# RetNet attention with a PReLU MLP on one core: a planner that counts TensorE's instruction chunks, three early transfers in flight, and 64-wide products with the sums

## The chip, the cores and the metric

The kernel runs on 1 core of a Trainium2 chip. The metric is the device time of one execution in microseconds. The engines are TensorE (PE; its weight loads are shown apart as PEld), VectorE (DVE), ScalarE (ACT), GpSimd (POOL) and SyncE (SP), which here issues the transfers between the chip's memory and the core.

## The reference, cut to what matters

```python
def _attn_ref(q, k, v):                    # each (8, 8, 576, 64): batch, heads, sequence, head size
    scores = 1.0 / np.sqrt(D_) * np.matmul(q, k.transpose(0, 1, 3, 2))
    gamma = 1.0 - 2.0 ** (-5.0 - np.arange(H))
    rel = pos[:, None] - pos[None, :]
    Dmat = np.where(rel >= 0, gamma[:, None, None] ** rel[None, :, :], 0.0)
    return np.matmul(scores * Dmat, v)

x = attn_out.transpose(0, 2, 1, 3).reshape(4608, 512)
h = x @ w_in                               # (512, 2048)
g = np.maximum(h, 0.0) + alpha * np.minimum(h, 0.0)
out = g @ w_out                            # (2048, 512)
```

Everything is float32.

## The kernel before

**Attention by chunks.** The sequence of 576 is cut into 9 chunks of 64. Inside a chunk, the scores of queries and keys are masked and multiplied with the values. Across chunks, the products of keys and values are summed into a running state for each head, and a chunk's queries are multiplied with the sum of all chunks before it. Two heads make a pair, since a head is 64 wide and an engine's tile has 128 rows.

**Two ways through the attention.** The first two of the eight batches are done in *parts*, all heads at once, while the machine starts: parts 0, 1, 2 are chunks 0 to 3, 4 to 7 and 8 of batch 0, and parts 3, 4, 5 those of batch 1. A part has these steps, each a function of the kernel:

- `load_part`: loads of k, q, v, 128 rows by 512 each (256 KB).
- `part_scale`: GpSimd scales q and v (L424).
- `part_transposes`: TensorE turns k and q (L448), ScalarE copies them out (L454).
- `part_scores`: 32 products of 64 x 64 on TensorE (L472), VectorE masks them (L478).
- `part_states`: 32 products of keys and values (L494), VectorE sums them up (L506, L508), and `part_carry` hands the last sum to the next part (L514).
- `part_values`: 32 products of masked scores and values (L541), then, added to the same two accumulators, the products with the sums (L557). These are cut into two halves of the head, so that each gives 32 rows: 64 products in parts 1 and 4, 48 in parts 0 and 3 (their first chunk has no sum before it). ScalarE copies the two accumulators into the x of the MLP (L572).
- Parts 2 and 5 have one chunk and go through `last_part` (L593 to L631).

The other six batches go pair by pair, 24 *joint steps* (`joint`), spread between the work of the MLP from 105 us on. TensorE's work in a joint step is: the values of the pair before in two pieces, `v0` and `v1` (L809, 18 products together); the last chunk's scores, `x` (L860, 2 products); and scores and states of the pair, `su` (L867 and L870, 32 products). `on_pe` gives them to the planner as the groups of `GROUPS`.

**The MLP.** Tokens go in 18 blocks of 256, hidden units in 8 groups of 256. The first eight cells (a block and a group) run in plain float32 (`unit_plain`, L1039, then `second_plain`, L1070). All others run as products of split pieces (`unit`, L1108; `unit_two`, L1138, two blocks at once; `second`, L1189), for which ScalarE, VectorE and GpSimd split x, g and the weights. Every product of plain float32 shows as two weight loads and two matmuls in the trace, a product of pieces or a transpose as one of each.

**Weights.** Each of 32 weight tiles of 512 KB is loaded, turned into float32 by ScalarE (L670, L672), VectorE (L680, L682, L691) and GpSimd (L694) in `convert`, and used from there.

**The order.** The code lists operations with `do(engine, cost, function, reads, writes, ...)`. `plan()` then makes the order: first backwards, for a due time of each operation, then forwards. There it takes, among operations of an engine that could start within `SLACK` of the earliest, the one that is due first. `SWITCH` is added where an operation's kind differs from the last one on the engine. The order is fixed by this plan; on the chip each engine runs its own list, with semaphores where one engine needs another's result. Costs change the order alone.

**Transfers.** All go through SP's queue, in the order of the plan (`dma`). For the operations that the plan puts into the first 100 us, a transfer on SP also waits until the bytes in flight before it, with its own, are under `IN_FLIGHT`: `5 << 18` bytes, five transfers of 256 KB.

Of the kernel before, what the change touches and what calls it, by code (L numbers as in the profile page):

```python
# [21 lines left out]
def kernel(  # L22
# [72 lines left out]
    a16 = const.tile([NFC, P], FP32, name="a16")  # L95
    malpha = const.tile([P, NFC], FP32, name="malpha")

    gam = [1.0 - 2.0 ** (-5.0 - h) for h in range(H)]
# [54 lines left out]
    class Op:  # L153
        def __init__(self, eng, cost, fn, deps, banks, late, lock, hold):
            self.eng, self.cost, self.fn, self.deps = eng, cost, fn, deps
            self.banks, self.late, self.lock, self.hold = banks, late, lock, hold
            self.n = len(ops)

# [17 lines left out]

    def do(eng, cost, fn, r=(), w=(), late=0.0, lock=False, kind=None, hold=0.0):
        deps, gens = set(), []
        for keys, writes in ((r, False), (w, True)):
            for g, *sub in keys:  # L180
                wr, rd = g.keys.setdefault(tuple(sub), ([], []))
                deps.update(wr)
                if writes:
                    deps.update(rd)
                deps.update(g.before)
                if g not in gens:
                    gens.append(g)
        op = Op(eng, cost, fn, None, [g.slot for g in gens if g.slot and g.slot.bank], late, lock, hold)
        for g, *sub in w:
            g.keys[tuple(sub)] = ([op], [])  # L190
        for g, *sub in r:
            g.keys[tuple(sub)][1].append(op)
        for g in gens:
            assert not g.slot or g.slot.gen is g
            g.ops.append(op)
        op.deps = [d for d in deps if d is not op]
        op.gens, op.kind = gens, kind or eng
        ops.append(op)
        return op
# [19 lines left out]
    flight, now = [], [0.0]  # L219
    LIMITED, IN_FLIGHT = 100.0, 5 << 18  # L220

    LAT = {"PE": 0.2}

    def plan():
# [42 lines left out]
        free, held, port, wire, kinds = dict(BEGIN), {}, [0.0, ""], 0.0, {e: e for e in BEGIN}  # L267
        can = [0.0] * len(ops)
        for op in ops:
            if not op.deps:  # L270
                ready[op.eng].append(op)

        def earliest(op):
            t = max(free[op.eng], can[op.n], op.hold)
            for b in op.banks:
                if b in held:
                    t = max(t, max([x + LAT.get(e, 0.1) for e, x in held[b].items()
                                    if e != op.eng] or [0.0]))
            if op.lock and port[1] != op.eng:
                t = max(t, port[0])  # L280
            if op.late:
                t = max(t, wire - BACKLOG, due[op.n] + last - HOLD)
            return t + SWITCH.get(op.eng, 0.0) * (kinds[op.eng] != op.kind)

        while len(order) < len(ops):
# [18 lines left out]
            kinds[op.eng] = op.kind  # L304
            free[op.eng] = end[op.n] = t + op.cost
            if op.late:
                wire = max(wire, t + op.cost) + op.late
                end[op.n] = wire
# [13 lines left out]

    AHEAD_PE = 150
    BACKLOG, HOLD = 2.0, 30.0
    LAG, HOLD_X = 2, 100.0
    PUMP0, PUMP = ((1, 1), (0, 1), (0, 1), (0, 1)), ((1, 2), (1, 2), (0, 1), (0, 1))
    GROUPS = (("v0",), ("v1",), ("x", "su"))
    SLACK, SWITCH = {"PE": 0.3}, {"PE": 0.1}
    BEGIN = {"PE": 3.8, "ACT": 0.5, "DVE": 5.5, "POOL": 5.4, "SP": 0.5}
# [106 lines left out]
    def part_transposes(x, i, bank):  # L436
# [6 lines left out]
        for m in range(2):  # L443
            pt = Gen(next(bank))

            def f(m=m, pt=pt):
                for c in range(NPAIR):
                    nc.tensor.transpose(pt.get()[:, c * P:(c + 1) * P],  # L448
                                        part(x, i)[:, m, 2 * c:2 * c + 2].rearrange(
                                            "p h d -> p (h d)"), ident)  # L450
            do("PE", 0.6 if x else 1.0, f, [key_p(x, i, m)], [(pt, 0)])

# [5 lines left out]
    def part_scores(x, bank):  # L458
# [7 lines left out]
        for m in range(2):  # L466
            def f(m=m):
                for c in range(NPAIR):
                    for p2 in range(2):
                        for h2 in range(2):  # L470
# [3 lines left out]
                                kT()[half(h2), c, j], qT()[half(h2), c, j], start=True, stop=True)  # L474
            do("PE", 0.6, f, [(kt, "t", m), (qt, "t", m)], [(ps[0], m), (ps[1], m)])
        for h2 in range(2):
# [7 lines left out]
    def part_states(x, bank):  # L484
# [4 lines left out]
        for m in range(2):  # L489
            def f(m=m):  # L490
                for c in range(NPAIR):
                    for p2 in range(2):
                        for h2 in range(2):
# [5 lines left out]
                                             skip_group_check=True)  # L499
            do("PE", 0.6, f, [key_p(x, 0, m), key_p(x, 2, m)], [(pu[0], 0), (pu[1], 0)])  # L500
        for j in range(4):
# [25 lines left out]
    def part_values(x, bank):  # L527
# [7 lines left out]
        for m in range(2):  # L535
            def f(m=m):
                for c in range(NPAIR):
                    for p2 in range(2):
                        for h2 in range(2):
# [5 lines left out]
                                             skip_group_check=True)  # L545
            do("PE", 0.6, f, [key_p(x, 2, m), (a, "m", 0), (a, "m", 1)], [(pv[0], 0), (pv[1], 0)])
        for m in range(2):
            js = [j for j in (2 * m, 2 * m + 1) if j or x % 3]

            def f(js=js):  # L550
                for j in js:
                    su = sums_of(x, j - 1) if j else carry_of(x)
                    for c in range(NPAIR):
                        for h2 in range(2):
                            for e in range(0, D, 32):
# [4 lines left out]
                                                 stop=(j >= 2), skip_group_check=True)  # L560
            do("PE", 1.0 if len(js) > 1 else 0.6, f, [(qt, "t", m)] + [
                sums_key(x, j - 1) if j else carry_key(x) for j in js], [(pv[0], 0), (pv[1], 0)])

# [15 lines left out]
    def last_part(x):  # L579
# [9 lines left out]
        def f():  # L589
            to = pt.get().rearrange("p (i c s) -> p i c s", i=2, c=NPAIR)  # L590
            for i in range(2):
                for c in range(NPAIR):
                    nc.tensor.transpose(to[:, i, c], part(x, i)[0:C, 0, 2 * c:2 * c + 2].rearrange(  # L593
                        "p h d -> p (h d)"), ident[0:C, 0:C])
        do("PE", 0.8, f, [key_p(x, 0, 0), key_p(x, 1, 0)], [(pt, 0)])
        do("ACT", 0.59, lambda: nc.scalar.copy(
# [6 lines left out]
        def f():  # L603
            for c in range(NPAIR):
                for h2 in range(2):
                    nc.tensor.matmul(sc(h2)[:, c], tt()[half(h2), 0, c], tt()[half(h2), 1, c],
                                     start=True, stop=True)
        do("PE", 0.5, f, [(t, "t")], [(ps[0], 0), (ps[1], 0)])
        for h2 in range(2):
# [5 lines left out]
        def f():  # L615
# [6 lines left out]
            for c in range(NPAIR):  # L622
                for h2 in range(2):
                    for e in range(0, D, 32):
# [3 lines left out]
                                         skip_group_check=True)  # L628
        do("PE", 0.9, f, [key_p(x, 2, 0), (t, "m", 0), (t, "m", 1), (t, "t"), carry_key(x)], [(pv, 0)])
        gx, o = chunk_home(x, NJ - 1)  # L630
# [203 lines left out]
    def on_pe(parts, groups):  # L834
        for some in groups:
            do("PE", sum(parts[x][0] for x in some), lambda some=some: [parts[x][1]() for x in some],
               [key for x in some for key in parts[x][2]],
               [key for x in some for key in parts[x][3]])

# [187 lines left out]
    def unit_plain(cell):  # L1027
# [5 lines left out]
        for cc in range(2):  # L1033
            def mm(cc=cc):
                w = plain[4 * u + cc]
                for f in range(2):
                    for c2 in range(2):
# [5 lines left out]
                                         stop=(cc == c2 == 1), skip_group_check=True)  # L1043
            do("PE", 1.75, mm, keys + [plain[4 * u + cc]], [(ph, 0)])
        do("ACT", 0.62, lambda: nc.scalar.activation(
# [10 lines left out]
    def second_plain(cell):  # L1056
# [9 lines left out]
        for m in range(2):  # L1066
            def mm(m=m, a=acc):
                for f in range(2):
# [4 lines left out]
                                     stop=(cell["last"] and f == 1))  # L1073
            do("PE", 1.75, mm, [(ga, 0), (ga, 1), plain[4 * u + 2], plain[4 * u + 3]],
               [(acc[m], 0)])
            if cell["last"]:
# [12 lines left out]
    def unit(cell):  # L1089
# [7 lines left out]
        for f in range(2):  # L1097
# [5 lines left out]
            def mm(f=f, at=at):  # L1103
# [7 lines left out]
            do("PE", 1.43, mm, x_keys(vis, side) +  # L1111
               [w_at[u, i][l] for i in range(2) for l in range(3)], [(ph, 0), (ph, 1)], kind="pieces")
            fc = 2 * u + f
# [14 lines left out]
    def unit_two(va, vb, u, ga, f):  # L1128
# [3 lines left out]
        def mm():  # L1132
# [7 lines left out]
        do("PE", 2.73, mm, x_keys(va, 0) + x_keys(vb, 1) +  # L1140
           [w_at[u, i][l] for i in range(2) for l in range(3)], [(p0, 0), (p1, 0)], kind="pieces")
        fc = 2 * u + f
# [31 lines left out]
    def second(cell):  # L1174
# [7 lines left out]
        for m in range(2):  # L1182

            terms = ((0, 0), (0, 1)), ((1, 2),)
            for some in reversed(terms) if cell["last"] else (sum(terms, ()),):
                def mm(m=m, a=list(acc), some=some):
# [8 lines left out]
                   [w_at[u, i][l] for i in (2, 3) for _, l in some],  # L1195
                   [(acc[2 * m + b], 0) for b in sorted({b for b, _ in some})], kind="pieces")
            if cell["last"]:
# [331 lines left out]
```

## Time and profile before

| what | us |
|---|---|
| median of 3 runs (lowest, highest) | 937.26 (936.19, 939.43) |
| the profiled execution's own time | 939.56 |
| its span, first to last instruction | 937.9 |
| TensorE idle before its first matmul | 4.24 |
| products of pieces with w_out, L1189: matmuls busy | 344.7 |
| products of pieces with w_in, L1108: matmuls busy | 208.7 |

Matmuls overlap, so their busy times are no sum of a time line. The profile's page gives busy time by engine, TensorE's granted clock and the share of the 16 DMA engines in 40 slices, the traffic of each DMA queue (q1 is the program's data, q8 and q14 fetch instructions), and the chain of work that ended last. "Issue" is a wait for which the profile has no releaser. In the page, DMA engines are busiest in the first 15% of the span:

```
DMA  9987487798888869965335421121212122221112
q1 hardware_dynamic: 235424, 119.59, 50.3%
q8 instruction: 65, 1.06, 0.5%
q14 instruction: 35, 0.29, 0.1%
```

The chain of work that ended last is 92% TensorE: 38% L1189, 21% L1108, 18% L1138.

### The profile page before, as it was taken

To read this page: it belongs to the slowest core of one execution; us is meant where nothing else is said; L and a number is where in the kernel's file an instruction comes from. 1 tells how busy PE (TensorE), PEld (TensorE's weight loads), DVE (VectorE), ACT (ScalarE), POOL (GpSimd) and SP (SyncE) were. 2 spreads that over 40 slices of the span, in tenths; PEclk is the share of its full clock that TensorE was granted. 3 is DMA by queue.
4 is the path that set the end of the run, shared out by engine and by line. 5 is a ranking of instruction groups with operands and counts; after the bars stand their busy time and mean duration, and the time that the engine had idled before them with its cause. 6 is when DMAs were issued, how large, how long until landed. Compare 5 with 4: busy or idle time off the path is not lost.

```text
span 937.9 us, 21264 instructions
## 1 busy us (share of the span) xinstructions
PE 915.6 (98%) x8241; PEld 778.5 (83%) x8241; DVE 531.9 (57%) x1070; ACT 552.8 (59%) x1175; POOL 578.8 (62%) x491
## 2 busy tenths in 40 slices
PE   6799999999999999999999999999999999999998
PEld 5576688988898898889899988888888888888887
DVE  6668566666776666766654764443444444444333
ACT  4366556566766665666775885645546463635342
POOL 5657766739676685664666465748374656647363
PEclk9999999999999999999999999999999999999999
DMA  9987487798888869965335421121212122221112
GB/s 233 226 200 137 131 197 159 157 205 188 196 189 197 204 152 196 196 148 151 113 113 191 125 90 68 46 90 45 90 45 91 58 89 88 78 71 45 45 45 68
DMA packets 235524, 120.94 MB, mean 129 GB/s; under 512 B 203408, under 2 KB 203424, under 8 KB 235424
## 3 DMA queue, kind: packets, MB, share of 16 engines
q1 hardware_dynamic: 235424, 119.59, 50.3%
q8 instruction: 65, 1.06, 0.5%
q14 instruction: 35, 0.29, 0.1%
HBM read 74.19 MB, written 31.98 MB: 113 GB/s over the span
## 4 chain that ended last, share of the span: by engine, by line
PE 92%; SPq 2%; DMA 2%; issue 1%; DVE 1%; POOL 1%; ACT 1%; POOLq 0%; ACTq 0%; DVEq 0%
PE pso L1189 38%; PE psh L1108 21%; PE psh L1138 9%; PE psa L1138 9%; PE psh L1039 3%; PE pso L1070 3%; PE psh L809 3%; SPq L206 2%; PE psa L870 2%; DMA op<-in_moe_w_out_dram 1%; DMA kn<-in_k_dram 1%; PE psh L860 1%; PE psa L867 1%; DMA w<-in_q_dram 1%; PE psa L472 0%
## 5 line engine op out<-in xcount | busy, mean ns | idle before, releaser
L1189 PE MATMUL pso<-w,g 128*128 128x512 f32 x1416 | 344.7, 391 | 0.0
L1189 PEld LDWEIGHTS pso<-w,g 128*128 128x128 f32 x1416 | 260.2, 188 | 50.6
L1108 PE MATMUL psh<-lx,w 128*128 128x256 f32 x1608 | 208.7, 285 | 0.0
L1108 PEld LDWEIGHTS psh<-lx,w 128*128 128x128 f32 x1608 | 202.0, 191 | 7.2 <-issue 0.5
L1168 POOL TENSOR_TENSOR g<-g 128x512 fp32r<-128x512 f32 x136 | 176.1, 1295 | 23.0 <-DVE w L1014 4.4
L1165 POOL TENSOR_TENSOR g<-ga,g 128x512 fp32r<-128x512 f32 x72 | 93.0, 1292 | 110.1 <-ACT g L1161 90.1
L1116 DVE SCALAR_TENSOR_TENSOR ga<-psh,ga 128x256 f32<-128x256 f32 x144 | 60.6, 421 | 67.5 <-ACT ga L1115 66.1
L1115 ACT COPY ga<-psh 128x256 f32<-128x256 f32 x144 | 53.6, 373 | 70.7 <-PE psh L1108 61.5
L1165 POOL TENSOR_TENSOR g<-x,g 128x512 fp32r<-128x512 f32 x40 | 51.7, 1294 | 63.8 <-ACT g L1161 61.3
L1122 DVE SCALAR_TENSOR_TENSOR ga<-psh,malpha,ga 128x256 f32<-128x256 f32 x144 | 68.9, 478 | 24.2 <-ACT psh L1119 23.4
L1018 POOL TENSOR_TENSOR lx<-lx 128x512 fp32r<-128x512 f32 x48 | 61.9, 1294 | 27.3 <-DVE lx L1014 12.7
L1119 ACT ACTIVATE psh<-ga 128x256 f32<-128x256 f32 x144 | 56.0, 389 | 28.0 <-DVE ga L1116 27.8
L1161 ACT ACTIVATE g<-ga 128x512 fp32r<-128x512 f32 x72 | 45.5, 632 | 25.0 <-DVE ga L1122 16.9
L1165 POOL TENSOR_TENSOR g<-vn,g 128x512 fp32r<-128x512 f32 x24 | 31.1, 1296 | 42.1 <-ACT g L1161 38.9
L888 DVE SCALAR_TENSOR_TENSOR at<-psa,pf,mask 64x512 f32<-64x512 f32 x48 | 36.0, 750 | 34.8 <-PE psa L867 33.9
L1163 ACT ACTIVATE g<-ga 128x512 fp32r<-128x512 f32 x72 | 45.0, 625 | 0.0
L1207 DVE TENSOR_TENSOR op<-pso,op 128x512 f32<-128x512 f32 x34 | 23.4, 687 | 36.5 <-PE pso L1189 36.4
L1161 ACT ACTIVATE g<-x 128x512 fp32r<-128x512 f32 x40 | 25.2, 632 | 32.0 <-PE pso L1189 16.1
L1145 DVE SCALAR_TENSOR_TENSOR x<-psh,x 128x512 f32<-128x512 f32 x20 | 13.8, 690 | 44.5 <-PE psh L1138 40.9
L809 PEld LDWEIGHTS psh<-at,vn 128*64 128x64 f32 x864 | 28.2, 137 | 12.6 <-issue 5.3
L1014 POOL TENSOR_TENSOR lx<-x,lx 128x512 fp32r<-128x512 f32 x24 | 31.0, 1294 | 12.2 <-DVE wa L682 6.2
L809 PE MATMUL psh<-at,vn 128*64 128x64 f32 x864 | 32.7, 226 | 2.5 <-DMA vn<-su 1.3
(289 smaller groups left out, 1695.5 us busy)
## 6 DMA issues: line engine op xcount, KB each, us to landing
xk<-x SPq DMA_DIRECT2D x18, 512.0 KB, 4.0
out_dram<-o SPq DMA_DIRECT2D x36, 256.0 KB, 4.2
ok<-o SPq DMA_DIRECT2D x34, 256.0 KB, 2.8
x<-xk SPq DMA_DIRECT2D x17, 512.0 KB, 5.0
op<-ok SPq DMA_DIRECT2D x17, 512.0 KB, 3.9
qx<-in_q_dram SPq DMA_DIRECT2D x96, 72.0 KB, 3.1
kx<-in_k_dram SPq DMA_DIRECT2D x96, 72.0 KB, 3.0
kn<-in_k_dram SPq DMA_DIRECT2D x48, 144.0 KB, 3.8
```

Source lines behind the costliest of these rows:

```text
L809: nc.tensor.matmul(pv[i].get()[half(h2), (j - js[0]) * C:(j - js[0] + 1) * C], vns[n % 2][:, h2, j], mt.get()[:, h2, j], start=True, stop= ...
L1018: lambda l=l, d=d, h=view(0, c): nc.gpsimd.tensor_tensor(out=piece(d()), in0=h(), in1=l(), op=ALU.subtract),
L1108: nc.tensor.matmul(at(b), w[:, c0:c0 + P], xp(l, cc), start=(n == 0 and cc == 0), stop=(n > 0 and cc == NCC - 1), skip_group_check=True)
L1115: do("ACT", 0.36, lambda g=g, at=at: nc.scalar.copy(g(), at(1)), [(ph, 1)], [(ga, f)])
L1116: do("DVE", 0.42, lambda g=g, at=at: nc.vector.scalar_tensor_tensor(out=g(), in0=at(0), scalar=ONE, in1=g(), op0=ALU.mult, op1=ALU.subtrac ...
L1119: do("ACT", 0.39, lambda g=g, at=at: nc.scalar.activation(at(1), g(), ACTF.Relu, scale=-1.0), [(ga, f)], [(ph, 1)])
L1122: do("DVE", 0.48, lambda g=g, at=at, fc=fc: nc.vector.scalar_tensor_tensor(out=g(), in0=at(1), scalar=malpha[:, fc:fc + 1], in1=g(), op0=A ...
L1138: nc.tensor.matmul(p.get(), w[:, c0:c0 + P], piece(words_of(g)[:, o:o + DM]), start=(l != 1 and cc == 0), stop=(l > 0 and cc == NCC - 1))
L1161: do("ACT", 0.64, lambda: nc.scalar.mul(piece(to.get()[:, 2]), whole(), BELOW), both, [(to, 2)])
L1165: do("POOL", 1.29, lambda: nc.gpsimd.tensor_tensor(out=piece(to.get()[:, 1]), in0=whole(), in1=to.get()[:, 2], op=ALU.subtract), both + [( ...
L1168: do("POOL", 1.29, lambda: nc.gpsimd.tensor_tensor(out=piece(to.get()[:, 2]), in0=to.get()[:, 0], in1=to.get()[:, 1], op=ALU.subtract), [( ...
L1189: nc.tensor.matmul(a[2 * m + b].get(), piece(g.get()[:, l, f, m * P:(m + 1) * P]), w_piece(u, 2 + f, l), start=(cell["first"] and f == 0 a ...
```

## The change

- The planner's forward pass gets a model of how TensorE's instructions arrive. Operations on TensorE carry a `size`, their number of matrix instructions. `at[0]` counts them modulo `CHUNK` = 256, beginning at 66; when an operation crosses a boundary, the next boundary may not be crossed before `FETCH` = 3.1 us (and up to 0.8 more while transfers are under way) have passed.
- Small products are a kind of their own (`kind="small"`), costs of several TensorE operations are set anew, and `SLACK` of TensorE goes from 0.3 to 0.2.
- `IN_FLIGHT` goes from `5 << 18` to `3 << 18`.
- In parts 1, 3 and 4 (`wide`), the products with the sums are no longer cut into halves of 32 rows: 32 products in parts 1 and 4, 24 in part 3. Before them ScalarE copies one row's two elements out of the accumulator that has the values (`spy`), and the first wide product waits for that copy, by a dependency added by hand.

```diff
+    spy = const.tile([1, 2], FP32, name="spy")
...
-    LIMITED, IN_FLIGHT = 100.0, 5 << 18
+    LIMITED, IN_FLIGHT = 100.0, 3 << 18
...
+        at = [CHUNK - 190, 0.0]
...
+            if op.size and at[0] + op.size > CHUNK:
+                t = max(t, at[1] - op.cost * (CHUNK - at[0]) / op.size)
             return t + SWITCH.get(op.eng, 0.0) * (kinds[op.eng] != op.kind)
...
+            if op.size:
+                at[0] += op.size
+                if at[0] >= CHUNK:
+                    at[0] -= CHUNK
+                    over = end[op.n] - op.cost * at[0] / op.size
+                    at[1] = over + FETCH + min(max(wire - over, 0.0), 0.8)
...
+    CHUNK, FETCH = 256, 3.1
...
-    SLACK, SWITCH = {"PE": 0.3}, {"PE": 0.1}
+    SLACK, SWITCH = {"PE": 0.2}, {"PE": 0.1}
...
-            do("PE", 0.6 if x else 1.0, f, [key_p(x, i, m)], [(pt, 0)])
+            do("PE", 0.52 if x else 1.0, f, [key_p(x, i, m)], [(pt, 0)], size=8)
...
-            do("PE", 0.6, f, [(kt, "t", m), (qt, "t", m)], [(ps[0], m), (ps[1], m)])
+            do("PE", 0.58, f, [(kt, "t", m), (qt, "t", m)], [(ps[0], m), (ps[1], m)], kind="small",
+               size=64)
...
+        wide = x > 0
+        if wide:
+            def f():
+                seen[:] = [nc.scalar.copy(spy[0:1], to(1)[0:1, NPAIR - 1, :, 0])]
+            seen = []
+            do("ACT", 0.2, f, [(pv[0], 0), (pv[1], 0)], [(pv[0], 1)])
         for m in range(2):
             js = [j for j in (2 * m, 2 * m + 1) if j or x % 3]
+
+            def g(js=js):
+                for c in range(NPAIR):
+                    for j in js:
+                        su = sums_of(x, j - 1) if j else carry_of(x)
+                        for h2 in range(2):
+                            ins = nc.tensor.matmul(
+                                to(j % 2)[half(h2 ^ (j % 2)), c, j // 2], su[half(h2), c],
+                                qT()[half(h2), c, chunk(j)], start=False, stop=(j >= 2),
+                                skip_group_check=True)
+                            if seen:
+                                tc.add_manual_dep(ins.ins, seen.pop().ins.name, mybir.DependencyInfo(
+                                    mybir.DependencyClass.Sync, mybir.DependencyReason.DATA),
+                                    reason="rows")
...
-            do("PE", 1.0 if len(js) > 1 else 0.6, f, [(qt, "t", m)] + [
-                sums_key(x, j - 1) if j else carry_key(x) for j in js], [(pv[0], 0), (pv[1], 0)])
+            do("PE", (0.29 if wide else 0.5) * len(js), g if wide else f, [(qt, "t", m)] + [
+                sums_key(x, j - 1) if j else carry_key(x) for j in js] + wide * [(pv[0], 1)],
+               [(pv[0], 0), (pv[1], 0)], kind="small", size=(32 if wide else 64) * len(js))
...
             do("PE", sum(parts[x][0] for x in some), lambda some=some: [parts[x][1]() for x in some],
                [key for x in some for key in parts[x][2]],
-               [key for x in some for key in parts[x][3]])
+               [key for x in some for key in parts[x][3]], kind="small",
+               size=sum(136 if x == "su" else 72 if x[0] == "v" else 0 for x in some))
...
-            do("PE", 1.75, mm, keys + [plain[4 * u + cc]], [(ph, 0)])
+            do("PE", 1.86, mm, keys + [plain[4 * u + cc]], [(ph, 0)], size=16)
...
-            do("PE", 1.75, mm, [(ga, 0), (ga, 1), plain[4 * u + 2], plain[4 * u + 3]],
-               [(acc[m], 0)])
+            do("PE", 1.86, mm, [(ga, 0), (ga, 1), plain[4 * u + 2], plain[4 * u + 3]],
+               [(acc[m], 0)], size=8)
```

The products of pieces get sizes of 24 (L1108, L1138) and 4 a term (L1189). Lines move by the added code; L448, L472, L494, L541, L557, L809, L1039, L1070, L1108 and L1189 of before are L461, L485, L508, L556, L597 (and the wide products L581), L851, L1082, L1113, L1151 and L1232 after; the copy is L570.

## The prediction

> **What bounds the kernel now.** I began with busy times and waits. TensorE is busy nearly throughout, and its waits are few, so the time is TensorE's own work plus its gaps.
>
> ```profile
> PE 915.6 (98%) x8241; PEld 778.5 (83%) x8241; DVE 531.9 (57%) x1070; ACT 552.8 (59%) x1175; POOL 578.8 (62%) x491
> ```
>
> ```profile
> PE psa L557 <- issue: 4.1, 1, 4.1
> PE psh L809 <- DMA vn<-su: 1.3, 1, 1.3
> PE psh L557 <- issue: 1.3, 1, 1.3
> ```
>
> The first line is the page's; the others are waits of the matmul engine. "Issue" is a wait that no semaphore explains. Both issue waits stand inside L557, the products with the sums. The chain of waits around the longer one, and then stretches of time (busy, matmuls, granted clock, DMA share, GB/s):
>
> ```profile
> 33.62 0.27 PE psh L557 x15
> 33.90 0.06 PE psh L557 x3
> 33.96 4.06 issue
> 38.02 0.48 PE psa L557 x20
> 38.67 0.33 PE psh L557 x22
> 39.00 3.61 PE psh L1039 x8
> ...
> 43.24 1.93 PE psh L1039 x8
> ```
>
> ```profile
> 39.00:42.40 3.40, 3.40 (x8) 0.50 0.96 240
> ...
> 86.00:92.00 6.00, 4.71 (x198) 1.00 0.55 100
> ```
>
> Two things are to be seen: 4.06 us of nothing, and after it eight matmuls in 3.61 us that take 1.93 four microseconds later, because the clock was 0.50 for 3.40 us. After the short wait at 89.94 the clock stayed 1.00.
>
> What TensorE waited for is told by the instruction queue: 65 packets with 1.06 MB, 16 KB each, for some 16,500 matrix instructions, so about 256 a packet. The engine counts up to the two waits are 602 + 602 and 1488 + 1489; their difference, 1773, and the 19 semaphore instructions of the program between them make 7 x 256. Both waits stand at such a boundary.
>
> ```profile
> q1 hardware_dynamic: 1164, 0.29, 125.3%
> q8 instruction: 1, 0.02, 5.7%
> ```
>
> These are the DMA queues at 35.2 to 36.6: the chunk's packet moves only there, with the data queue full. One chunk earlier the boundary fell at 31.9 (third matrix instruction of L541). From crossing to going on took 6.1 us (31.9 to 38.02), and TensorE had 2.0 us of small products for it. At 88.2 it took 3.0 (88.23 to 91.23), with the data queue at 20.6%, against 1.7 us of products.
>
> **The change, part by part.**
>
> *Counting chunks.* I laid the same boundaries (every 256 instructions, first at the 194th) on the changed order. No chunk there is pure small products. The densest in the disturbed stretch holds 11 instructions of L508, 4 matmuls of L1082 (1.83 us, half of the 16-matmul row of 3.65), all of L556 (128 instructions, 1.09 us) and 99 of L581 (0.85), with the new wait (0.6) inside: 4.5 us. That is above 3.0 and below 6.1. I take the wait as gone (the nearest row, with fewer loads in the way, is 3.0): -4.06 and -1.29. With it goes the half clock, half of 3.40: -1.7. If the fetch still takes 6.1, 1.6 us stay.
>
> The Trainium skill speaks against this: "Runtime: NRT & Kernel Launch", section on instruction fetch mechanics, calls the fetch of a 16 KiB block mostly hidden, so counting would bring nothing. The trace shows two waits at just these boundaries, and it decides. "TensorE: Matmul & The Clock Gate", Part 1, says an idle window of some 3.4 us halves the clock; our rows agree for 4.06 (0.50) and for 1.29 (1.00), and the 1.7 us are from the rows.
>
> *64-wide products.* 11 blocks (4 + 3 + 4) go from 16 products of 32 columns to 8 of 64; each is two matmuls. L557 in part 3 ran undisturbed: 96 matmuls in 1.32 us (63.83 to 65.15), 13.75 ns each. A 64x64 product in the same four quarters is L541: 64 in 1.09, 17 ns. So 352 x 13.75 = 4.84 becomes 176 x 17 = 2.99: -1.85. Other bound: L619, 64x64 in two quarters, 16 in 0.61 us, 38 ns: 6.7 us, +1.85. I take the first, same shape and same quarters but for one operation.
>
> *The new copy and wait.* In parts 3 and 4 the changed order puts two products of L1113 (1.91 us) between L556 and the wide products; they hide the copy. In part 1 the wide products stand straight behind L556: TensorE, with everything in its queue, waits for the copy. A small ScalarE copy is 0.2 us, plus two hand-overs of 0.1 to 0.2: +0.6 (0.3 to 1.0). Without the cover, parts 3 and 4 would cost the same each.
>
> *Order of the rest.* The added sizes and kinds, the smaller slack and the new costs run no instruction, but they move TensorE's operations for the whole kernel. The count gives 72 to each of the two halves of the values (L851), which together are 18 products of two matmuls, 72 instructions. The planner so sees 280 instructions in a joint step of 208, and puts other work inside. In the changed order TensorE enters the joint products from the split-precision ones 33 times after the first, now 26. The price of an entry, from the chain:
>
> ```profile
> 144.61 3.12 PE psh L1108 x24
> 147.73 2.75 PE pso L1189 x12
> 150.47 2.87 PE psh L1108 x24
> ...
> 156.09 1.20 PE psh L809 x36
> ```
>
> ```profile
> 196.31 0.73 PE psh L809 x20
> ...
> 198.24 0.62 PE psh L809 x16
> ```
>
> From start to next start in the timeline, 24 matmuls of L1108 behind joint products take 2.97 (118.47) to 3.02 (144.54), else 2.87: 0.13 on the mean. L1189 before them lasts 2.84, else 2.75: 0.09. Values in two pieces take 0.73 + 0.62, in one 1.20: 0.15. Sum 0.37; 7 x 0.37 = +2.6. Early, the plain units are entered 22 times, now 19; L1070 before small products takes 1.91, between transposes 1.72: 3 x 0.19 = +0.6.
>
> *Three transfers in flight.* A 256 KB load alone took 3.3 us, the next ones 4.0, 4.6 and 4.8, and they landed 1.19 apart. With three allowed, a turn is the longer of 3 x 1.19 = 3.57 and 3.3 + 0.4 (issue, 0.43 on SP): 3.7 us for 786 KB, 212 GB/s; before it averaged 235 in 0 to 33.96. All on SP shift: the fourth load, now behind the first landing (4.11), lands 0.3 later, about 8.0, and the last transposes of part 0 with it; weights behind it by 2 us, which VectorE's and ScalarE's queue meets with its own wait for the sums (L506 at 15.3). In part 1 the last block of q lands near 24, its scaling (1.04) waits behind POOL's conversions until 25.5, and TensorE waits 1.2 for it; but 2.4 us of waits in the same stretch now (0.33 for L454, 0.66 for malpha, 1.07 for the masked scores, 0.33 for x) partly go, since 16 transposes stand together. I take +0.5, between -1.5 (the waits go) and +9 (priced below).
>
> *Sum:* -4.06 - 1.7 - 1.29 - 1.85 + 0.6 + 2.6 + 0.6 + 0.5 = -4.6. The profiled execution has a span of 937.9 and took 939.56, above the median of 937.26 (936.19 to 939.43); so 933.3 in the span and **932.7** for the median.
>
> **Rivals.**
>
> *A, the stall stays in part (18%).* For it: the fetch of 31.9 stood in a full data queue, and three loads still fill it. The chunk of 4.5 us then leaves 1.6 idle. Idle of 1.29 did not halve the clock, 4.06 did; with 1.7 for the clock, -4.6 + 3.3 = -1.3: 936.0. Against it: fewer packets in front of it.
>
> *B, the window starves TensorE (12%), slower.* Place: states of part 1 (L508), which need the 23rd transfer, 6.3 MB into the stream. TensorE would be there near 32 us; 6.3 MB at 212 GB/s plus 2 is 31.7. It decides from 3.7 us a load on. If a load takes 4.5 even with three in flight (the page's median for k), a turn is 4.9, 160 GB/s: 41 us, 9 late: 932.7 + 9 = 941.7. Against it: the first load's 3.3, and weights that landed 0.7 apart.
>
> *C, more is gained (12%).* The split values hide the 1.3 us for vn<-su and the 1.0 for ga, and the start gains 1.5 instead of losing 0.5: -4.3 more, 928.4.
>
> **How the numbers follow.** The forecast holds 58%, from -2.5 to -6.5. No change is within 0.3% (2.8 us; 934.4 to 940.1), about what a measurement can tell. Faster: 53 of the forecast's 58, 11 of C, 1 of A: 65. Same: 5 of the forecast, 15 of A, 1 each of B and C: 22. Slower: 11 of B, 2 of A: 13. The range takes the forecast and most of A and C: 928.8 to 937.6; the likeliest alone 930.8 to 934.8.
>
> **What would show it.** Issue waits of L581 gone, clock 1.00 after the start; 96 and 128 wide-product instructions in 0.8 and 1.1 us; a wait of 0.6 on L570's copy in part 1 alone; L1151 at 3.1 seven times more often. Waits of TensorE for k, q, v or converted weights above 3 us before 45 us would be B; an issue wait near 36 us would be A. The forecast is wrong if TensorE's gaps before 110 us add up to more than now, 15.7 with the first 4.2.

## The result, and the profile after

| | median, us (runs) | ratio to the kernel before, 95% interval |
|---|---|---|
| before | 936.67 (17) | |
| after | 941.16 (17) | 1.0046 [1.0033, 1.006] |

The changed kernel is slower by 4.5 us. The forecast was 932.7. The profiled execution of after took 942.04 with a span of 940.3, 0.9 above its median; that of before stood 2.9 above its own median, so the two traces are 2.5 us apart, not 4.5.

First the lines that answer to those of before: busy times from the page, then TensorE's waits (us in total, times, longest), then stretches of time (length, busy, matmuls, granted clock, DMA share, GB/s).

```profile
PE 920.1 (98%) x8065; PEld 778.8 (83%) x8065; DVE 532.0 (57%) x1070; ACT 551.8 (59%) x1178; POOL 579.2 (62%) x491
```

```profile
PE psh L1082 <- ACT x L613: 2.5, 1, 2.5
PE psh L1082 <- POOL lx L736: 1.6, 1, 1.6
PE psa L556 <- DVE w L523: 1.6, 1, 1.6
...
PE psa L581 <- ACT spy L570: 0.3, 1, 0.3
```

```profile
20.40:23.80 3.40, 3.40 (x10) 0.50 0.75 171
37.50:40.90 3.40, 3.40 (x16) 0.50 0.78 159
68.20:71.60 3.40, 3.40 (x22) 0.50 0.66 166
86.00:92.00 6.00, 6.00 (x81) 1.00 0.82 153
```

What is to be seen: both issue waits of before are gone. Three waits stand in their place, at 16.89, 35.6 and 65.3, and each has a half-clock stretch of 3.4 us behind it, where before had one such stretch. The wait for the spy copy is there in part 1 alone, 0.3 and not 0.6.

The trace is one execution, and three such stretches are not the rule. One stretch of 3.41 us at half clock takes 0.0018 off the mean granted clock, which is on record for each of the 17 executions: 0.994 for this one, 0.996 or 0.997 for five, 0.998 for eight, 1.000 for three.

By stage, from TensorE's instructions ("waits" are its idle gaps behind its first matmul, "joint" from the first joint step to the first product of two blocks):

| profiled execution | first joint step at | waits before it | half-clock stretches before it | joint | waits in joint | rest |
|---|---|---|---|---|---|---|
| before | 104.95 | 11.4 | 1 | 451.9 | 2.5 | 381.0 |
| after | 106.66 | 10.5 | 3 | 453.2 | 1.7 | 380.5 |

Before the first joint step the waits became shorter by 0.9 us, but two more half-clock stretches cost 2 x 1.7 = 3.4 us; the first warm-up of the clock was some 0.7 us cheaper. That makes +1.8; +1.7 was measured. In the joint stretch the waits fell by 0.8 and TensorE's work grew by 2.1.

What the new waits wait for is told by the engines' own lists. ScalarE in after, from the timeline (start, duration, engine, line, operation; idle time before it and its releaser in brackets), and the same in a kernel that differs in the number of transfers in flight alone (five; the first experiment below):

```profile
15.19 0.68 ACT L712 ACTIVATE qT<-lx 128x512 f32<-128x512 f32 x1 [1.83 <-DMA lx<-in_moe_w_in_dram]
...
17.50 1.75 ACT L613 COPY x<-pso 128x512 f32<-128x512 f32 x3
```

```profile
16.01 0.67 ACT L714 ACTIVATE lx<-lx 128x512 int32<-128x512 uint32 x1
17.41 1.77 ACT L613 COPY x<-pso 128x512 f32<-128x512 f32 x3 [0.73 <-PE pso L597]
```

The copies L613 hand the x of part 0 to TensorE's L1082. They stand behind weight conversions (L712, L714). In after one of these waits 1.83 us for its load. TensorE is done with its products (L597) at 16.4, but ScalarE can start the copies only at 17.50. With five in flight ScalarE is through with the weights at 16.7 and waits for TensorE. This first wait costs next to nothing beside five, though: there TensorE came to L597 1.4 us later (its clock rose at 14.11, in after at 10.17), and the copies start at 17.41, hardly earlier.

At 35.6 TensorE waits for converted weights themselves. VectorE's and GpSimd's steps of that conversion in after, then with five:

```profile
32.53 0.69 DVE L722 TENSOR_SCALAR psa<-w 128x512 f32<-128x512 f32 x1 [2.65 <-ACT w L712]
...
35.87 1.29 POOL L736 TENSOR_TENSOR lx<-lx,w 128x512 int32<-128x512 int32 x1 [2.29 <-DVE lx L733]
```

```profile
27.99 0.69 DVE L722 TENSOR_SCALAR psa<-w 128x512 f32<-128x512 f32 x1 [0.20 <-ACT w L712]
...
31.81 1.29 POOL L736 TENSOR_TENSOR lx<-lx,w 128x512 int32<-128x512 int32 x1 [1.59 <-issue]
```

VectorE has to wait 2.65 us for ScalarE's part (L712) and begins 4.5 us later than with five, GpSimd's last step (L736) 4.1 us later. TensorE is 0.9 us later before this wait and 3.5 behind it.

At 65.3 it waits for the sums of part 3 (L521, L523), which stand on VectorE behind conversions (L722, L724, L733):

```profile
58.13 0.66 ACT L712 ACTIVATE w<-w 128x512 f32<-128x512 f32 x1 [2.14 <-POOL w L437]
...
58.83 0.69 DVE L722 TENSOR_SCALAR psa<-w 128x512 f32<-128x512 f32 x1 [5.47 <-ACT w L712]
...
65.33 0.42 DVE L521 COPY w<-psa 128x256 f32<-128x256 f32 x1
...
66.88 0.33 PE L556 MATMUL psa<-at,w 64*64 64x64 f32 x4 [1.59 <-DVE w L523]
```

```profile
51.02 0.67 ACT L712 ACTIVATE w<-w 128x512 f32<-128x512 f32 x1
...
51.72 0.69 DVE L722 TENSOR_SCALAR psa<-w 128x512 f32<-128x512 f32 x1 [3.85 <-ACT w L712]
...
58.23 0.42 DVE L521 COPY w<-psa 128x256 f32<-128x256 f32 x1
```

From L722 to L521 VectorE takes 6.5 us in both, without a pause; what differs is when it can begin. In after a load of w_in lands at 58.06 and ScalarE's L712 starts at 58.13, with five at 51.02. The products that L521 reads were done by 63.4 (L508 in the timeline); TensorE needs their accumulator again for the next values (L556) and waits until 66.9.

TensorE's plain products (L1082, L1113) come in the same order in both kernels, so each can be set against itself:

| TensorE starts | after | five in flight | later by |
|---|---|---|---|
| first L1082, behind the wait at 16.89 | 19.39 | 19.33 | 0.06 |
| first of the eight L1082 before the wait at 35.6 | 31.70 | 30.76 | 0.94 |
| next L1082, behind that wait | 37.21 | 33.67 | 3.54 |
| next L1113, behind the half-clock stretch | 43.30 | 38.40 | 4.90 |
| an L1082 before the wait at 65.3 | 60.75 | 55.90 | 4.86 |
| an L1113 behind it | 68.56 | 61.31 | 7.25 |
| an L1082 behind the half-clock stretch | 74.02 | 65.28 | 8.74 |
| first joint step | 106.66 | 97.09 | 9.57 |

So 7.8 of the 9.6 us come between 31 and 74 us, with the waits at 35.6 and 65.3 and the clock behind them; 0.9 come with the clock behind the first wait, and 0.8 later.

### The profile page after: what moved, and what is told of

Same layout as the page of the kernel before. It is cut to its first block, busy times and chain, and to the rows that moved or that the text cites. A ratio compares the mean times of both kernels' runs of the same rounds, so it can differ in the third digit from the quotient of the medians.

```text
span 940.3 us, 20910 instructions
## 1 busy us (share of the span) xinstructions
PE 920.1 (98%) x8065; PEld 778.8 (83%) x8065; DVE 532.0 (57%) x1070; ACT 551.8 (59%) x1178; POOL 579.2 (62%) x491
## 4 chain that ended last, share of the span: by engine, by line
PE 52%; DVE 0%; issue 0%
PE pso L1232 26%; PE psh L1181 9%; PE psa L1181 9%; PE psh L1151 7%; DVE o L1255 0%; PE psh L851 0%
## 5 line engine op out<-in xcount | busy, mean ns | idle before, releaser
L1232 PE MATMUL pso<-w,g 128*128 128x512 f32 x1416 | 346.0, 392 | 0.0
L1232 PEld LDWEIGHTS pso<-w,g 128*128 128x128 f32 x1416 | 260.0, 188 | 51.0
L1151 PE MATMUL psh<-lx,w 128*128 128x256 f32 x1608 | 208.6, 285 | 0.9 <-ACT x L870 0.9
L1151 PEld LDWEIGHTS psh<-lx,w 128*128 128x128 f32 x1608 | 202.2, 191 | 8.0 <-ACT x L870 1.0
L851 PEld LDWEIGHTS psh<-at,vn 128*64 128x64 f32 x864 | 28.3, 137 | 12.0 <-issue 4.7
L1181 PE MATMUL psh<-w,w 128*128 128x512 f32 x144 | 34.6, 389 | 0.0
```

The lines of the kernel that those rows point to most:

```text
L1151: nc.tensor.matmul(at(b), w[:, c0:c0 + P], xp(l, cc), start=(n == 0 and cc == 0), stop=(n > 0 and cc == NCC - 1), skip_group_check=True)
L1181: nc.tensor.matmul(p.get(), w[:, c0:c0 + P], piece(words_of(g)[:, o:o + DM]), start=(l != 1 and cc == 0), stop=(l > 0 and cc == NCC - 1))
L1232: nc.tensor.matmul(a[2 * m + b].get(), piece(g.get()[:, l, f, m * P:(m + 1) * P]), w_piece(u, 2 + f, l), start=(cell["first"] and f == 0 a ...
```

## The experiments

Each ratio is against the kernel before on the same chip (medians 936.91, 935.75 and 936.35 in the three groups, the first two on one chip); a difference to after or to five in flight is one of medians. The kernel before itself moved by 1.2 us between groups, so where two kernels stand in different groups, about 1 us can't be told.

**Five in flight again.** The order of the plan does not depend on the window, so this undoes that part alone.

```diff
-    LIMITED, IN_FLIGHT = 100.0, 3 << 18
+    LIMITED, IN_FLIGHT = 100.0, 5 << 18
```

> The changed kernel with five transfers in flight again; every engine runs the same instructions in the same order. Theory W (the window of three makes the weights late, and with them the conversions that stand in order on ScalarE, VectorE and GpSimd): the waits of 2.50 us at 16.9, 1.60 at 35.6 and 1.59 at 65.3 go or halve, two of the three half-clock stretches of 3.4 us go (1.7 us each), and the median comes to 933 to 937, 4 to 8 us under the changed kernel's 941.2. Theory O (the new order and its splits cost the time, whatever the window): the waits stay where they are and the median is 940 to 942. Theory F (the window is what makes the instruction fetch short): issue waits of more than 1 us are back inside the wide products.

Measured: 931.24 (930.72 to 932.14), ratio 0.9944 [0.993, 0.9957]: 9.9 us under after, more than theory W asked for. Its waits before and behind the first joint step; only the first of the three is left, smaller:

```profile
PE psh L1082 <- ACT x L613: 1.4, 1, 1.4
PE psh L851 <- DVE ga L1165: 0.8, 1, 0.8
```

The first joint step starts at 97.09 (waits before it 5.2 us, no half-clock stretch behind the warm-up). Of the 9.6 us to after's 106.66, 5.3 are waits, and the three half-clock stretches make up to 5.1; the longer first warm-up with five (to 14.11, not 10.17) takes some of it off. No issue wait came back (theory F falls), and O falls. The cause is to be read in the first three stretches of 20 us, in after and with five:

```profile
0.00:20.00 20.00, 10.21 (x308) 1.00 0.79 201
20.00:40.00 20.00, 17.48 (x182) 0.85 0.76 202
40.00:60.00 20.00, 19.72 (x319) 0.98 0.86 207
```

```profile
0.00:20.00 20.00, 11.82 (x308) 1.00 0.99 232
20.00:40.00 20.00, 19.01 (x314) 1.00 1.06 233
40.00:60.00 20.00, 20.00 (x265) 1.00 1.01 265
```

With three in flight the DMA engines have a share of 0.76 to 0.86, with five about 1. The mean is 203 GB/s against 243; over 60 us that leaves the stream 60 x (1 - 203/243) = 9.9 us behind. The 44th load of the list lands at 62.25, with five at 53.63. It is the limit that holds the stream back, and not engines that free buffers late: in the first 62 us SP waits 37 us for the landings of earlier transfers and 0.3 for engines, with five 13 and 5. ScalarE meets the late loads: its waits for weight loads before the first joint step (us in total, times, longest), in after and with five:

```profile
ACT w L712 <- DMA w<-in_moe_w_in_dram: 8.1, 4, 3.2
ACT w L712 <- DMA w<-in_moe_w_out_dram: 7.6, 7, 2.1
```

```profile
ACT w L712 <- DMA w<-in_moe_w_out_dram: 2.8, 2, 2.2
ACT w L712 <- DMA w<-in_moe_w_in_dram: 2.7, 2, 2.5
```

**Three in flight on the kernel before**, the same edit the other way round.

> The kernel before with three transfers in flight, nothing else; every engine runs the same instructions in the same order. Theory W (three in flight make weights and parts late whatever the order): new waits of TensorE before 75 us of 4 to 8 us in all, and 942 to 947. Rival N (the window hurts only the new order, which has no slack left for late loads): 936 to 938. Rival Q (the instruction fetch at 31.9 took 6.1 us because the data queue was full, and three in flight free it): the issue wait of 4.06 falls under 2 us and the time to 932 to 934.

Measured: 945.15 (943.98 to 946.04), 1.0082 [1.0058, 1.0106], 9.4 us more. The window costs the old order as much as the new one: W, and not N. (Its trace, 1.1 us under its median, is only 4.5 us over that of before, 2.9 above its own.) On the mean the granted clock takes 4.7 us of its six executions and 1.1 of before's. The trace's waits (it has one half-clock stretch, at 83.3):

```profile
PE psa L448 <- DMA w<-in_k_dram: 5.7, 2, 4.3
PE psa L494 <- DVE w L478: 3.8, 2, 2.1
PE psa L557 <- issue: 2.6, 1, 2.6
PE psh L557 <- issue: 1.2, 1, 1.2
```

Here TensorE also waits for a load of k itself, 1.4 us at 18.2 (the 4.3 are the start) and 1.1 at 22.0. The fetch wait is 2.6 in this trace, 4.1 in that of before, and not under the 2 us of Q: the smaller window does not end it.

**Four, and six, in flight on after** (`4 << 18`, `6 << 18`).

> The changed kernel with four transfers in flight. Theory W with a load's own time as the limit (3.0 to 3.6 us a load with three in flight, so 3 x 262 KB a turn): four in flight are limited by the landings, 1.19 us apart, and no longer by a load's own time, so most of the loss goes: 931 to 934. Rival: each transfer taken from the window costs the same, half of 9.9: 936.

> The changed kernel with six transfers in flight. Theory W: with five the DMA engines were already at shares of 0.99 to 1.06 in the first 60 us (0.79, 0.76 and 0.86 with three), so a sixth only waits longer in the queue: 930 to 932.5. If the instruction fetch suffers from a fuller queue: issue waits above 1 us before 105 us, and 933 or more. If transfers still are what TensorE waits for: under 930.

Measured: four 934.94 (933.05 to 937.19), 0.998 [0.9963, 0.9998]; six 930.97 (929.83 to 932.23), 0.9937 [0.9914, 0.996]. Three, four, five and six give 941.2, 934.9, 931.2 and 931.0: the gain ends where the engines' share comes to 1 (four: 0.89, 0.96, 0.95; six: 1.02, 1.02, 1.01). Four came between the two expectations, with 6.2 of the 9.9 us gained: most of the loss, as W has it, but 3.7 us are left.

**Three for the first 30 us only, and after 30 us only**, by the plan's time.

```diff
-                    if eng == "SP" and ahead >= IN_FLIGHT:
+                    if eng == "SP" and ahead >= (IN_FLIGHT if now[0] < 30.0 else 5 << 18):
```

The second has the two values exchanged.

> The changed kernel with three transfers in flight for what the plan puts before 30 us, and five after it. Of the 9.9 us between three and five, the wait of 2.50 at 16.9 (1.36 with five) and its half-clock stretch stand before 30 us: 1.1 + 1.7 = 2.8. If a wait belongs to the loads that were held back just before it: 931.2 + 2.8 = 934. If what is lost early is never made up (the whole stream stays behind): the waits at 35.6 and 65.3 stay, 939 to 941.

> The same the other way round: five in flight before 30 us, three after. If a wait belongs to the loads held back just before it: the waits at 35.6 and 65.3 and their two half-clock stretches stay, 1.6 + 1.6 + 3.4 = 6.6, and 938. If the early loads decide: 931 to 933.

Measured: 935.54 (934.53 to 938.62), 0.9995 [0.998, 1.001], and 935.36 (933.18 to 937.69), 0.9981 [0.9966, 0.9997]. Each half costs about 4.2 us, 8.4 of the 9.9 together. That the early loads decide everything falls. But a wait does not belong to the loads just before it alone either: with three before 30 us a wait of 1.3 us is left at 36 and one of 0.8 at 69.

All of these keep TensorE's order up to the first joint step (so does the kernel with other sizes, below). Their traces follow the rate of the first 60 us:

| in flight | GB/s in 0 to 60 us | share | 60 x (1 - GB/s / 243) | first joint step later than with five | median over five |
|---|---|---|---|---|---|
| three (after) | 203 | 0.80 | 9.9 | 9.6 | 9.9 |
| three (other sizes) | 211 | 0.86 | 7.9 | 7.3 | 8.3, over five with these sizes |
| three, then five | 229 | 0.91 | 3.5 | 3.9 | 4.3 |
| five, then three | 229 | 0.93 | 3.5 | 2.3 | 4.1 |
| four | 229 | 0.93 | 3.5 | 2.7 | 3.7 |
| six | 245 | 1.01 | -0.5 | -0.4 | -0.3 |

**The old costs, kinds and slack, with five in flight.** The order of the plan without the count is the same for TensorE up to the first joint step. The new costs, kinds and slack are what moved it there. This run takes those back and keeps the count and the wide products.

```diff
-    SLACK, SWITCH = {"PE": 0.2}, {"PE": 0.1}
+    SLACK, SWITCH = {"PE": 0.3}, {"PE": 0.1}
...
-            do("PE", 0.52 if x else 1.0, f, [key_p(x, i, m)], [(pt, 0)], size=8)
+            do("PE", 0.6 if x else 1.0, f, [key_p(x, i, m)], [(pt, 0)], size=8)
...
-            do("PE", 1.86, mm, keys + [plain[4 * u + cc]], [(ph, 0)], size=16)
+            do("PE", 1.75, mm, keys + [plain[4 * u + cc]], [(ph, 0)], size=16)
```

and so for the other costs, with `kind="small"` left out.

> The changed kernel with five in flight and with the old costs, no kind for small products and the old slack; the count of chunks and the wide products stay. TensorE's order before the first joint step is another one, in which one chunk (the fifth) holds nothing but small products and 8 matmuls: 108 instructions of L556, 128 of L581, some 2.9 us of work. Theory C (the new costs and kinds, not the count, spread the small products and so took the fetch waits away): an issue wait of 1 to 3 us in that stretch and 934 to 938. Rival (order and kinds bring nothing; the wide products and the window are all there is): 931 to 932.5.

Measured: 933.47 (932.34 to 934.65), 0.9965 [0.9952, 0.9978], 2.2 us more than with the new costs, between the two expectations. An issue wait is back, as theory C said, though in the products of part 0 (L597) and not in the chunk that I had named:

```profile
PE psh L461 <- POOL w L437: 2.2, 1, 2.2
PE psh L1151 <- DVE ga L1165: 1.9, 1, 1.9
PE pso L597 <- issue: 1.4, 1, 1.4
```

So in these traces the new costs and kinds take a fetch wait away, and with it a share of the 2.2 us that can't be told from the other waits of this order. The two kernels stand in different groups, but all their executions lie apart (932.34 and more, 932.14 and less).

**No count, with five in flight.**

```diff
-            if op.size and at[0] + op.size > CHUNK:
+            if False:
```

> The changed kernel with five in flight, and the planner's forward pass without the test that holds an operation back for an instruction chunk. Up to the first joint step not one TensorE instruction moves; after it TensorE enters the joint products 29 times, not 33. If the count brings nothing: no issue wait anywhere, and 4 x 0.37 = 1.5 us less in the stretch from the first joint step to the first product of two blocks, 929.7 in all. If the count keeps fetch waits away in that stretch: issue waits appear there, and the time is 931.2 or more.

Measured: 931.37 (seven executions from 929.92 to 933.41; an eighth took 3185 us and does not count), 0.9942 [0.9919, 0.9965]. No issue wait anywhere. So the count, which gives the change its name, brings nothing that can be seen with five in flight; with three it was not run. The joint stretch is 451.6 against 452.7 with five, and without its waits 449.9 against 451.4, the 1.5 expected; the median does not show it.

**The right number of instructions for the values**, alone and with five in flight.

```diff
-               size=sum(136 if x == "su" else 72 if x[0] == "v" else 0 for x in some))
+               size=sum(136 if x == "su" else 8 * round(parts[x][0] / 0.133) if x[0] == "v" else 0 for x in some))
```

> The changed kernel, but the planner is told 8 matrix instructions for each chunk of values (72 for both halves together) and not 72 for each half. Up to the first joint step the order stays as it is; after it TensorE enters the joint products from the split-precision ones 29 times, not 33. With the forecast's 0.37 us an entry: 1.5 us less, 939.7, and the stretch from the first joint step to the first product of two blocks 1.5 us shorter than 453.2. If entries cost nothing: 941.2 and the same stretch.

> Both: five in flight, and 8 matrix instructions a chunk of values. The two act in different stretches (before 105 us and after), so the gains should add: theory W with entries at 0.37 us gives 931.5 to 935.5, below the kernel before (936.7); theory O gives 939 to 941.

Measured: 939.65 (936.73 to 941.73), 1.0028 [1.0015, 1.0041], and 931.33 (929.3 to 934.0), 0.9944 [0.9927, 0.9961]. The joint stretch without its waits is 449.6 and 449.9, against 451.5 and 451.4 with 33 entries and 449.4 in before with 26. Four entries less are 1.5 to 1.9 us of TensorE's work. In the median that shows with three in flight (-1.5, though the two intervals against before overlap) and not with five (+0.1), where waits of that stretch took a part back in the trace (2.0 us against 1.3). Nothing is settled on a gain of 1.5 with five.

**Narrow products with the sums**, with three and with five in flight.

```diff
-            do("PE", (0.29 if wide else 0.5) * len(js), g if wide else f, [(qt, "t", m)] + [
+            do("PE", (0.29 if wide else 0.5) * len(js), f, [(qt, "t", m)] + [
```

> The changed kernel with the products with the sums cut in halves of 32 rows again, in the place of the wide ones; the order is the same, and the small ScalarE copy stays, with nothing waiting for it. By the forecast's term the products take 4.84 us and not 2.99: 943.0, unless the longer products fill a wait that is there anyway. If the wide products gain nothing beside their wait for the copy: 941.2 or less. If the wide products make the fetch wait again (fewer instructions in a chunk's time), the narrow ones are faster than 940.

> The changed kernel with five in flight and the products with the sums in halves of 32 rows, in the same order. With TensorE hardly waiting (5.2 us of waits before the first joint step, against 10.5 in the changed kernel) the forecast's term is to be seen undiluted: 931.2 + 1.85 = 933.1. Where the 0.81 us seen with three in flight is all there is: 932.0. Where the narrow products bring a fetch wait back, as in the kernel before: an issue wait above 1 us in L597 and 934 or more.

Measured: 941.97 (939.54 to 944.71), 1.0061 [1.0043, 1.008], with three, and 934.84 (931.55 to 938.7), 0.9977 [0.996, 0.9995], with five. With three nothing can be told (0.8 us, intervals overlap). With five the narrow products cost 3.6 us, in different groups; the two traces are 2.9 apart. TensorE's busy time with these products alone (length of the stretch, busy, matmuls, granted clock, DMA share, GB/s), the wide ones and then the narrow ones, both with five in flight:

```profile
36.00:42.00 6.00, 1.16 (x64) 1.00 1.07 239
62.00:66.00 4.00, 1.15 (x48) 1.00 0.96 227
80.00:86.00 6.00, 1.16 (x64) 1.00 0.32 51
```

```profile
36.00:42.00 6.00, 1.71 (x128) 1.00 1.01 231
62.00:68.00 6.00, 1.40 (x96) 1.00 0.96 172
82.00:88.00 6.00, 1.73 (x128) 1.00 0.56 102
```

4.84 - 3.47 = 1.4 us are the products. Issue waits of 1.1 (L1082, at 66) and 0.4 us (L597) are in the narrow kernel's trace and not in the other's; with three in flight the narrow kernel's trace has none. Together that is 2.9 us. It is no full account: the narrow kernel's waits before the first joint step are longer by only 0.7 us in all (6.0 and 5.3), and it has a half-clock stretch at 18.7 that the other has not. That the wide products, with fewer instructions for the same work, spare fetches is one trace's word.

## Why the prediction was wrong, step by step

**The step that failed** is the term "Three transfers in flight", +0.5. It is +9.9 on the new order and +9.4 on the old one. Put in place of the +0.5, it turns the sum of -4.6 into +4.8; measured +4.5. It lies outside even the bounds that were given for the term, -1.5 to +9. Three things in it were off:

- *The rate, a little.* "A turn is ... 3.7 us for 786 KB, 212 GB/s". The 203 GB/s of the first 60 us make it 786/203 = 3.87 us. Rival B, with its "it decides from 3.7 us a load on", held by its own number, and I had set the turn just on it.
- *What a lower rate does over time.* I carried the shift to "weights behind it by 2 us" and the last block of q, around 24 us, and stopped there. A stream that is 16% slower falls further behind as long as it is the bound, and with five in flight the DMA engines are busy throughout the first 60 us (shares 0.99 to 1.06): 9.9 us at the end. Part 0, the only place in which late weights were looked for, ended up 0.06 us later (19.39 against 19.33); the bill came at 35 and 65 us.
- *What covers it.* "VectorE's and ScalarE's queue meets with its own wait for the sums" named a wait of before as cover. But the conversions stand in a fixed order ahead of sums that TensorE needs, so at 65 us a late load holds back work that has nothing to do with it; and at 35 us the converted weights were themselves late.

Rival B had the mechanism, a starved TensorE, and the wrong place. That its price is so close (941.7; it is 941.16) is luck: it came from loads of 4.5 us, 160 GB/s and one wait of 9 us, and none of these was measured. TensorE never waited for v at L508: the 23rd transfer landed at 32.5, near the 31.7 that I worked out. The waits are for converted weights, or for work behind conversions, in three places, but each is under the 3 us set for "converted weights" in "What would show it". Against B I had held single loads (3.3 us, and weights 0.7 apart). With three in flight the single load did get faster, mostly 3.0 to 3.8 us, while the stream got slower; so the reason for giving B only 12% did not bear on it.

**The test at the end was the wrong one.** The forecast was to be wrong if the gaps before 110 us became more than 15.7. They are 14.8 with the first 4.3, less than before, and the kernel is slower: the test counted waits and not the clock behind them, though the sum itself had a term for the clock.

**Fetch waits, -4.06 and -1.29: gone in the trace, for another reason.** The heading was "Counting chunks", and the count moved nothing there. New costs, kinds and slack spread the small products, and narrow or differently ordered ones have issue waits of 0.4 to 1.4 us. What the two waits cost in a median execution of before no run shows; they were read from one that took 2.9 us more.

**Half clock, -1.7: right for its place in the trace**, but three stretches came elsewhere with the three waits, two more than before. Over all executions the granted clock on record costs 2.3 us on the mean in after and 1.1 to 1.8 in the three groups of before, so it brought a loss and no gain. Of the 71 executions of before in these groups, 34 have a clock of 0.999 or more, too much for even one such stretch: the term was not there to be won in each.

**Wide products, -1.85: mis-sized**; the products take 1.4 us less in the trace. 48 matmuls take as long as 64 (1.15 and 1.16), so 17 ns each does not hold for the smaller group. In the medians, with whatever waits they spare, they are worth 3.6 us with five in flight.

**The copy and its wait, +0.6: 0.3**, in part 1 alone, as said. **Entries into the joint products, +2.6: 2.1** (451.5 - 449.4 without waits, 7 entries, 0.30 each instead of 0.37). The +0.6 for plain units was not measured by itself. Without the term for the window the sum is -5.1, and the kernel without the window is -5.7 against before. That these agree is in part luck. The wide products and their copy were to bring 1.25 us and brought 3.6; all the rest was to bring 3.85, and the kernel with five in flight and narrow products, which has all the rest, is only 0.9 under before.

**What stays open.** The trace of after has three half-clock stretches, and that of the kernel with other sizes, which has the same order up to there, has one (first joint step at 104.4). On the mean the granted clock takes 2.3 us in after and 0.6 with five, so some 2 of the 9.9 us are clock and the rest is not; what the executions of after at a clock of 1.000 (940.36, 941.16 and 942.22) waited for has no trace. Which cost or kind took the fetch wait away was not tried one by one.

## What to carry to other kernels

When a limit on transfers is tightened, ask first whether the DMA engines were full in that stretch. If their share is near 1, a limit that keeps them below it can cost that share of the whole stretch, and not the delay of one load; three, four, five and six in flight cost 9.9, 3.7, 0 and 0 us here, against five. And set the same instruction of two traces side by side before a wait is called a loss: the longest of the new waits, 2.5 us, ended 0.06 us later than with five. A load that lands late costs what stands behind its consumer in that engine's list, so follow the list of every engine that converts or copies, not only the tile's own user. And of a change with several parts, price each on its own: all but the window was worth 5.7 us here, and the window took 9.9 away.

## What the runs showed of the hardware

**Half a window of idle was enough to halve TensorE's clock.** In all 14 traces the clock's stretches after the start are multiples of 3.41 us (3.4, 6.8, 10.2, 13.7, 27.3), as if it were set anew at fixed times. I laid windows of that length on these times and summed TensorE's idle time in each. Wherever at least 1.82 us of a window were idle, the next one ran at 0.50 (7 of 7). With at most 1.48 us it never did; between 1.62 and 1.75 it did in three of six. So the same wait can cost 1.7 us more or nothing, by where it falls: with five in flight, the 1.38 us of the narrow kernel at 17.73 began in a window that with shorter gaps before it held 1.62 us of idle, and a half-clock stretch came; the 1.36 us of the wide kernel at 17.97, behind the same instructions, were alone in their window, and none came. Full speed came back only after a window with at most 0.45 us idle (0.42 was twice not enough yet); after one with 1.0 (four in flight, from 18.9) the clock stayed at half for another.

The Trainium skill, "TensorE: Matmul & The Clock Gate", Part 1, says that the window is free-running and 3413 ns long, with which these stretches agree. It gives one idle window as what brings the clock down; here half of one was enough, and the measurement decides. My reading of its rule, that 1.29 us are harmless and 4.06 are not, left out everything between.

**Fewer transfers in flight make each faster and all slower.** Loads of 256 KB took mostly 3.0 to 3.8 us in the first 35 us with three in flight where they took 4 to 6 with five, and the rate of the first 60 us fell from 243 to 203 GB/s (on the kernel before from 232 to 205).
